# Five unread products around the first query products, an eight-fold Sinkhorn matrix, and a clearing that moves to a later round

## The chip, the cores and the metric

The kernel runs on one core of a Trainium2 chip. The metric is the device time of one execution in microseconds (us); the number given for a kernel is the median of its runs.

## The reference, cut to what matters

Four batches of eight heads, 768 positions, 64 values per head; `sort_net` holds one 8 by 8 matrix per batch and head.

```python
P = sort_net                                   # (4, 8, 8, 8)
for _ in range(5):
    P = exp(P - max(P, -1))
    P = P / (sum(P, -1) + 1e-9)
    P = P / (sum(P, -2) + 1e-9)
k_sorted = einsum('bhij,bhjcd->bhicd', P, k_blocks)     # 8 blocks of 96 positions
v_sorted = einsum('bhij,bhjcd->bhicd', P, v_blocks)
attn = softmax(q_blocks @ k_sorted.T / 8)               # 96 x 96 inside each block
x = (attn @ v_sorted)  ->  (3072, 512)
out = (silu(x @ w_gate) * (x @ w_val)) @ w_out          # 512 -> 1536 -> 512
```

## The kernel before, in words

The kernel has a short, latency-bound start and a long part in which TensorE (PE) works through the feed-forward blocks. Most of the order on PE, VectorE (DVE), ScalarE (ACT) and GpSimd (POOL) is the order in which the source issues the instructions: the start is under a manual schedule for these four, the rest under one for PE, POOL, ACT and SyncE.

**Sinkhorn** (L217 to L237). The 32 matrices lie on 32 partitions, `p_ps` is a tile in PSUM. A round is: the exponential on ACT (L219), then on DVE the row sum (L229), its reciprocal, the product (L231), the column sum (L232), its reciprocal, the product (L235). Each step needs the one before it, so DVE waits for ACT once in every round. Extra DVE and ACT work is put between the exponential and the row sum: the reduction to `mask` in the second round (L222), copies of V on ACT in the second to fourth (L223 to L227). In the last round the closing product writes `p_bf` (L236), a bf16 copy of the matrix, repeated four times along the free dimension. `vt_tile(pair)` (L192) allocates the tile for a pair of batches' mixed values and clears one column of it to 1.0 (L195); both tiles are made ahead of Sinkhorn.

**The mixing matrix** (L488 to L505). For each of the 8 output blocks, four products with a 32-column slice of `p_bf` as the stationary operand and the identity as the moving one write the transposed matrix to the four groups of 32 PSUM partitions of `w_ps` (L492). DVE multiplies it with `mask` into `rmix[0]` (L497) and copies the rest to `w_sb` (L502), from which POOL makes the other batches' `rmix`.

**Batch 0 on PE.** Ahead of `w_ps`, PE runs `wide_fill` (L481), fp32 products of zeros that nobody reads, with one tiny product between them that waits for a copy of V (L484), and then `q0_chunk(0, 0, 8)` (L274), the transposition of the first query pieces, which waits for their load. Behind `w_ps` come the other query pieces, the value products `v_chunk` (L300) and the key products `k0_chunk` (L284). Each of them fills one or two PSUM banks, which DVE or ACT then empties into SBUF (`drain`, L242 and L244). PSUM banks come from three rings: "gen" with three banks of 512 columns, "x" with one, and "a" and "b" with a pair each. Then follow scores (`qk`, L332) with the exponential on ACT (`e_all`, L345 and L343), `av` (L359) with its normalisation on DVE (L363, L365), the transposition of the result (L376), and the first gate and value products `early` (L557).

**The feed-forward blocks.** `ffn(n)` runs `gate` (L410), `value` (L428) and, for the block before, `outp` (L445); `merge` places the attention of later batches between them by fixed due times.

**Loads.** POOL issues them in program order: the first values, queries and keys, then its own copies of V into `vch` (L150), then the gate and value weights in pieces (`load_gv`, L136), then batch 1's keys, queries and values (L102) and the output weights (L514), then four more copies into `vch` for batch 1 (L150 again).

The fill that the start uses elsewhere, and that the change adds, is

```python
def fill(tile, n):
    for _ in range(n):
        nc.tensor.matmul(tile, lhsT=warm_sb[:, 0:128], rhs=warm_sb, start=True, stop=True)
```

where `warm_sb` is a 128 by 512 bf16 tile of zeros.

Of the kernel before, what the change touches and what calls it, by code (L numbers as in the profile page):

```python
# [10 lines left out]
BF16 = mybir.dt.bfloat16  # L11
AF = mybir.ActivationFunctionType
ALU = mybir.AluOpType
# [4 lines left out]
def kernel(  # L18
# [11 lines left out]
    nc = tc.nc  # L30

    B, H, S, D = q.shape
    NB = sort_net.shape[-1]
    C = S // NB
    BH = B * H
# [18 lines left out]
    const = ctx.enter_context(tc.tile_pool(name="const", bufs=1))  # L54
# [40 lines left out]
    def grouped(t):  # L95
        return t[:, :, 0:GC * D].rearrange("p s (c d) -> p s c d", d=D)

    def dense(t):
        return t.rearrange("p s n -> p (s n)")[:, 0:C * D].rearrange("p (c d) -> p c d", d=D)
# [42 lines left out]
    def copy_v(eng, pair, rows, s, n=4, d0=0, d1=D, cs=None):  # L142
        cs = cs or slice(s * (C // n), (s + 1) * (C // n))
        dst = vch3[rows, d0:d1, cs]
        src = (dense(v_tiles[0])[rows, cs, d0:d1] if rows == lowr else
               grouped(v_tiles[pair])[rows, s, :, d0:d1])
        if eng is nc.scalar:
            eng.copy(dst, src.transpose([0, 2, 1]))
        else:
            eng.tensor_copy(dst, src.transpose([0, 2, 1]))  # L150
# [41 lines left out]
    def vt_tile(pair):  # L192
        if pair not in vts:
            t = vtp.tile([C, 2, H * NB, D + 8], BF16, name=f"vt{pair}", tag="vt")
            nc.vector.memset(t[:, :, :, D:D + 1].rearrange("p u n e -> p (u n) e"), 1.0)  # L195
            vts[pair] = t
        return vts[pair]

    for pair in range(B // 2):
        vt_tile(pair)  # L200

    mask = const.tile([128, H], BF16)
    sel = const.tile([128, 2, H2, 16], BF16)
# [1 line left out]

    rowreds = [const.tile([BH, NB, 1], FP32, name=f"rowred{it}") for it in range(N_ITER)]
    colred = const.tile([BH, 1, NB], FP32)
    p_bf = const.tile([BH, NB, 4, NB], BF16)
    w_sb = const.tile([128, NB, B, H], BF16)
    pad = const.tile([1, 16], FP32)  # L210
    def pair_tile(name, tag):
# [2 lines left out]
    def bank_tile(name, tag="gen"):  # L214
        return psum.tile([128, 512], FP32, name=name, tag=tag, bufs=3 if tag == "gen" else 1)

    p_ps = bank_tile("p_ps")[0:BH, 0:NB * NB].rearrange("p (i j) -> p i j", j=NB)  # L217
    for it in range(N_ITER):
        nc.scalar.activation(p_ps, p_sb if it == 0 else p_ps, AF.Exp)  # L219
        if it == 1:  # L220
            with nc.allow_low_precision("0/1 mask"):
                nc.vector.tensor_reduce(mask, id4, axis=AX.XY, op=ALU.add)  # L222
            nc.scalar.copy(sel, ident.rearrange("p (r g two) -> p two g r", g=H2, two=2))  # L223
        if it == 2:
            copy_v(nc.scalar, 0, lowr, 0, cs=slice(24, 34))
        if it == 3:
            copy_v(nc.scalar, 0, lowr, 0, cs=slice(34, 46))  # L227
        rowred = rowreds[it]
        nc.vector.reduce_sum(rowred[:, :, 0], p_ps, axis=AX.X)  # L229
        nc.vector.reciprocal(rowred, rowred)  # L230
        nc.vector.tensor_mul(p_ps, p_ps, rowred.to_broadcast([BH, NB, NB]))  # L231
        nc.vector.reduce_sum(colred[:, 0, :], p_ps.transpose([0, 2, 1]), axis=AX.X)  # L232
        nc.vector.reciprocal(colred, colred)
        if it < N_ITER - 1:
            nc.vector.tensor_mul(p_ps, p_ps, colred.to_broadcast([BH, NB, NB]))  # L235
    nc.vector.tensor_tensor(p_bf, p_ps.unsqueeze(2).to_broadcast([BH, NB, 4, NB]),  # L236
                            colred.unsqueeze(1).to_broadcast([BH, NB, 4, NB]), op=ALU.mult)  # L237
    copy_v(nc.scalar, 0, lowr, 0, d1=40, cs=slice(46, 72))

    def drain(eng, dst, src):  # L240
        if eng == "v":
            nc.vector.tensor_copy(dst, src)  # L242
        else:
            nc.scalar.copy(dst, src)  # L244
# [3 lines left out]
    def kqt_tile(b):  # L248
        if b not in kqts:
            kqts[b] = kqp.tile([128, 2 * H2 * NB * C + 32], BF16, name=f"kqt{b}", tag="kqt")  # L250
        return kqts[b]
# [3 lines left out]
    def chunk_tile(name, n, tag):  # L255
        return pair_tile(name, tag) if n == 2 else bank_tile(name, tag)
# [12 lines left out]
    def q0_chunk(t, at, n, eng, tag):  # L269
        dst = kqt_tile(0)[:, GI * C:2 * GI * C].rearrange("p (g t r c) -> p t g r c", g=H2, t=2, c=QC)[:, t]  # L270
        tp = chunk_tile("tq0", n // 8, tag).rearrange("p (l g r) -> p l g r", l=n, g=H2)
        for lc in range(n):
            for two in range(2):
                nc.tensor.matmul(tp[two * D:(two + 1) * D, lc], lhsT=q0[t][:, at + lc, :],  # L274
                                 rhs=sel[:, two], start=True, stop=True)
        drain(eng, dst[:, :, :, at:at + n], tp.rearrange("p l g r -> p g r l"))
# [196 lines left out]
    idle_ps = bank_tile("idle_ps", "x")  # L473
# [5 lines that stand above are left out]
    def wide_fill(n):  # L479
        for _ in range(n):  # L480
            nc.tensor.matmul(idle_ps, lhsT=wide_sb[:, 0:128], rhs=wide_sb, start=True, stop=True)  # L481

    wide_fill(3)
    nc.tensor.matmul(idle_ps[0:8, 0:8], lhsT=vch[lowr, 24:32], rhs=vch[lowr, 24:32], start=True, stop=True)  # L484
    wide_fill(1)
    q0_chunk(0, 0, 8, "s", "x")

    w_ps = bank_tile("w_ps")[:, 0:NB * B * H].rearrange("p (i b h) -> p i b h", b=B, h=H)  # L488

    for i in range(NB):  # L490
        for g in range(4):
            nc.tensor.matmul(w_ps[32 * g:32 * g + 32, i].rearrange("p b h -> p (b h)"),  # L492
                             lhsT=p_bf[:, i].rearrange("p a b -> p (a b)"),
                             rhs=ident[0:BH, 0:BH], start=True, stop=True)

# [39 lines left out]
    idle_ps = bank_tile("idle_ps", "x")  # L535
# [159 lines left out]
```

## Time and profile before

| | |
|---|---|
| median of 3 runs | 245.98 us (245.24 to 246.05) |
| the profiled execution | 245.7 us, of which the span from first to last instruction is 243.9 us |
| PE busy | 235.5 us, 97% of the span |
| DVE, ACT, POOL busy | 155.6, 112.1, 54.6 us |
| mean granted clock of PE | 0.984 |

Times inside the profile count from the start of the span. "Idle before" is the time that an engine stood still ahead of an instruction, with what ended the wait. "PEclk" is the clock that PE was granted, as a share of the full one. A matmul's row includes the tail after its last column went in, so that two rows in sequence overlap a little; the spacing of a group is read from the chain of waits, which counts no time twice.

### The profile page before, as it was taken

To read this page: it belongs to the slowest core of one execution; us is meant where nothing else is said; L and a number is where in the kernel's file an instruction comes from. 1 tells how busy PE (TensorE), PEld (TensorE's weight loads), DVE (VectorE), ACT (ScalarE), POOL (GpSimd) and SP (SyncE) were. 2 spreads that over 40 slices of the span, in tenths; PEclk is the share of its full clock that TensorE was granted. 3 is DMA by queue.
4 is the path that set the end of the run, shared out by engine and by line. 5 is a ranking of instruction groups with operands and counts; after the bars stand their busy time and mean duration, and the time that the engine had idled before them with its cause. 6 is when DMAs were issued, how large, how long until landed. Compare 5 with 4: busy or idle time off the path is not lost.

```text
span 243.9 us, 5926 instructions
## 1 busy us (share of the span) xinstructions
PE 235.5 (97%) x2487; PEld 138.5 (57%) x2487; DVE 155.6 (64%) x327; ACT 112.1 (46%) x190; POOL 54.6 (22%) x66
## 2 busy tenths in 40 slices
PE   7598999999999999999999999999999999999994
PEld 3296666676555565555655555565556555555543
DVE  6668789876664585867755845574675576445700
ACT  3958654476635544455553452254325334332312
POOL 5997229970006089000000000000000000000000
PEclk9959999999999999999999999999999999999999
DMA  5989999999936998643121212012111211110122
GB/s 95 216 119 186 207 212 213 206 212 197 161 89 101 218 173 101 127 97 78 46 75 37 60 57 78 1 59 63 32 43 46 75 36 43 43 43 3 43 86 86
DMA packets 40698, 24.76 MB, mean 102 GB/s; under 512 B 29408, under 2 KB 35424, under 8 KB 40672
## 3 DMA queue, kind: packets, MB, share of 16 engines
q0 software_dynamic: 20688, 14.16, 39.9%
q1 hardware_dynamic: 19840, 10.17, 16.0%
q8 instruction: 19, 0.31, 0.5%
q10 hardware_dynamic: 144, 0.07, 0.1%
q14 instruction: 7, 0.06, 0.1%
HBM read 28.32 MB, written 7.86 MB: 148 GB/s over the span
## 4 chain that ended last, share of the span: by engine, by line
PE 92%; DVE 4%; ACT 1%; DMA 1%; issue 1%
PE v_ps L428 25%; PE g_ps L410 25%; PE o_ps L445 25%; PE av_ps L359 3%; PE tkq L264 3%; PE qk L332 3%; PE tv L300 2%; PE tk L284 1%; PE tv L310 1%; PE o_ps L461 1%; PE tq L274 1%; DMA p_sb<-in_sort_net_dram 1%; PE g_ps L557 1%; DVE st L365 1%; PE x_ps L376 1%
## 5 line engine op out<-in xcount | busy, mean ns | idle before, releaser
L420 DVE SCALAR_TENSOR_TENSOR gs_sb<-th_sb,g_ps 128x384 bf16<-128x384 bf16 x96 | 52.9, 551 | 50.0 <-ACT th_sb L418 46.9
L410 PE MATMUL g_ps<-xt,wg_sb 128*128 128x384 bf16 x376 | 76.6, 326 | 0.1
L428 PE MATMUL v_ps<-xt,wv_sb 128*128 128x384 bf16 x376 | 76.5, 326 | 0.0
L418 ACT ACTIVATE th_sb<-g_ps 128x384 bf16<-128x384 f32 x96 | 47.1, 491 | 56.8 <-PE g_ps L410 54.1
L445 PE MATMUL o_ps<-wo,h 128*128 128x512 bf16 x276 | 64.4, 379 | 0.0
L433 DVE SCALAR_TENSOR_TENSOR h<-v_ps,gs_sb 128x384 bf16<-128x384 f32 x96 | 53.4, 556 | 7.7 <-DVE gs_sb L420 0.5
L410 PEld LDWEIGHTS <-wg_sb 128*128 128x128 bf16 x376 | 34.8, 97 | 23.4
L428 PEld LDWEIGHTS <-wv_sb 128*128 128x128 bf16 x376 | 35.0, 97 | 23.1 <-issue 0.2
L445 PEld LDWEIGHTS <-h 128*128 128x128 bf16 x276 | 26.0, 98 | 28.5
L450 ACT COPY o_sb<-o_ps 128x512 f32<-128x512 f32 x23 | 13.5, 586 | 49.3 <-PE o_ps L445 46.3
L150 POOL COPY vch<-v 64x1536 bf16<-64x1536 bf16 (+2 forms) x11 | 29.1, 2688 | 9.9 <-DMA v<-in_v_dram 9.9
L345 ACT ACTIVATE e_all<-qk 96x768 bf16<-96x768 f32 x30 | 23.2, 801 | 3.8 <-PE qk L332 3.7
L365 DVE TENSOR_TENSOR st<-av_ps,r_sb 96x512 bf16<-96x512 f32 x32 | 21.7, 680 | 0.3
L359 PEld LDWEIGHTS <-e_all 96*128 96x128 bf16 x256 | 11.9, 97 | 4.6 <-ACT e_all L345 0.3
L359 PE MATMUL av_ps<-vt,e_all 96*128 96x65 bf16 x256 | 13.0, 193 | 0.2 <-ACT e_all L345 0.2
L244 ACT CAST vt<-tv 96x1024 bf16<-96x1024 f32 (+1 forms) x10 | 9.7, 965 | 5.9 <-PE tv L310 3.5
L363 DVE RECIPROCAL r_sb<-av_ps 96x8 f32<-96x8 f32 x32 | 6.3, 198 | 7.8 <-PE av_ps L359 7.8
L242 DVE CAST vt<-tv 96x1024 bf16<-96x1024 f32 (+1 forms) x8 | 8.1, 1017 | 3.1 <-PE tv L310 1.8
L481 PE MATMUL idle_ps<-wide_sb 128*128 128x512 f32 x8 | 6.6, 977 | 1.5 <-DVE wide_sb L70 1.5
L242 DVE COPY oq_v<-o_ps 128x128 f32<-128x128 f32 x1 | 0.3, 291 | 9.3 <-PE o_ps L461 9.3
L300 PE MATMUL tv<-rmix,vch 64*128 64x64 bf16 (+1 forms) x128 | 5.8, 208 | 0.0
L300 PEld LDWEIGHTS <-vch 64*128 64x128 bf16 (+1 forms) x128 | 5.4, 107 | 0.6
(87 smaller groups left out, 132.9 us busy)
## 6 DMA issues: line engine op xcount, KB each, us to landing
out_dram<-o_sb SPq DMA_DIRECT2D x23, 256.0 KB, 2.0
v<-in_v_dram POOLq DMA_DIRECT2D x4, 384.0 KB, 11.8
wo<-in_moe_w_out_dram POOLq DMA_DIRECT2D x3, 512.0 KB, 17.3
kqp<-in_k_dram POOLq DMA_DIRECT2D x2, 768.0 KB, 10.7
q_scr<-in_q_dram POOLq DMA_DIRECT2D x2, 768.0 KB, 18.1
v<-in_v_dram POOLq DMA_DIRECT2D x2, 768.0 KB, 9.8
wg_sb<-in_moe_w_gate_dram POOLq DMA_DIRECT2D x2, 512.0 KB, 12.0
wv_sb<-in_moe_w_val_dram POOLq DMA_DIRECT2D x2, 512.0 KB, 14.2
```

The costliest lines, as they stand in the source:

```text
L150: eng.tensor_copy(dst, src.transpose([0, 2, 1]))
L300: nc.tensor.matmul(tp[:, ld, :], lhsT=vch[rows, col:col + 128], rhs=mix, start=True, stop=True)
L345: nc.scalar.activation(e_all[:, n:n + 2, 0:4 * C], wide[0:C, :, 0:4 * C], AF.Exp, scale=scale)
L359: nc.tensor.matmul(o[:, two, i4, 0:D + 1], lhsT=e[:, i4 * C:i4 * C + 128], rhs=vt[:, 2 * g + two, half * 4 + i4, 0:D + 1], start=True, sto ...
L365: nc.vector.tensor_tensor(st.rearrange("p i two d -> p two i d"), o[0:C, :, :, 0:D], r_sb.to_broadcast([C, 2, 4, D]), op=ALU.mult)
L410: nc.tensor.matmul(g_ps, lhsT=wg_sb[:, kc, ts(m, 128)], rhs=xt[:, kc, :], start=(kc == 0), stop=(kc == NKC - 1))
L418: nc.scalar.activation(th_sb, g_ps, AF.Tanh, scale=0.5)
L420: nc.vector.scalar_tensor_tensor(gs_sb, th_sb, 1.0, g_ps, op0=ALU.add, op1=ALU.mult)
L428: nc.tensor.matmul(v_ps, lhsT=wv_sb[:, kc, ts(m, 128)], rhs=xt[:, kc, :], start=(kc == 0), stop=(kc == NKC - 1))
L433: nc.vector.scalar_tensor_tensor(h_tiles[n][:, m, :], v_ps, 0.5, gs_tiles.pop(m), op0=ALU.mult, op1=ALU.mult)
L445: nc.tensor.matmul(o_ps, lhsT=h_w[:, m, ts(t3, 128)], rhs=wo_sb[part][:, m % 4, :], start=(m == 0), stop=(m == NFC - 1))
L450: nc.scalar.copy(o_sb, o_ps)
```

## The change

Three edits, all in the start. Three products of 512 columns are issued on PE ahead of the first query products and two behind them, the latter into a bank of the "gen" ring; nobody reads what they write. `p_bf` holds the matrix eight times instead of four, so a stationary operand has 64 columns, and each output block takes two products that write 64 partitions each instead of four that write 32. The tile for the second pair of batches is made, and its column cleared, in Sinkhorn's third round and no longer ahead of the first.

```diff
-    for pair in range(B // 2):
-        vt_tile(pair)
+    vt_tile(0)
...
-    p_bf = const.tile([BH, NB, 4, NB], BF16)
+    p_bf = const.tile([BH, NB, 8, NB], BF16)
...
         if it == 2:
             copy_v(nc.scalar, 0, lowr, 0, cs=slice(24, 34))
+            vt_tile(1)
...
-    nc.vector.tensor_tensor(p_bf, p_ps.unsqueeze(2).to_broadcast([BH, NB, 4, NB]),
-                            colred.unsqueeze(1).to_broadcast([BH, NB, 4, NB]), op=ALU.mult)
+    nc.vector.tensor_tensor(p_bf, p_ps.unsqueeze(2).to_broadcast([BH, NB, 8, NB]),
+                            colred.unsqueeze(1).to_broadcast([BH, NB, 8, NB]), op=ALU.mult)
...
     wide_fill(1)
+    fill(idle_ps, 3)
     q0_chunk(0, 0, 8, "s", "x")
+    fill(bank_tile("idle_ps"), 2)
...
     for i in range(NB):
-        for g in range(4):
-            nc.tensor.matmul(w_ps[32 * g:32 * g + 32, i].rearrange("p b h -> p (b h)"),
+        for g in range(2):
+            nc.tensor.matmul(w_ps[64 * g:64 * g + 64, i].rearrange("p b h -> p (b h)"),
                              lhsT=p_bf[:, i].rearrange("p a b -> p (a b)"),
                              rhs=ident[0:BH, 0:BH], start=True, stop=True)
```

## The prediction

> **What bounds the kernel now.** I read the page first, then the granted clock by stretches, then the chain that ended last, then the timelines of DVE, PE and POOL in the first 50 us. The page:
>
> ```profile
> span 243.9 us, 5926 instructions
> ...
> PE 235.5 (97%) x2487; PEld 138.5 (57%) x2487; DVE 155.6 (64%) x327; ACT 112.1 (46%) x190; POOL 54.6 (22%) x66
> ...
> PEclk9959999999999999999999999999999999999999
> ```
>
> TensorE (PE) is busy nearly throughout, so time that is taken out of the start reaches the end unless a later load stops it. The one odd digit is the 5 in the third slice of the clock. The windows view, cut at the clock's own steps, shows it (columns: stretch, its length, then busy time and count of PE, PEld, DVE, ACT, POOL, then granted clock, DMA share, GB/s):
>
> ```profile
> 7.54:10.95 3.41, 1.66 (x19) 0.71 (x19) 2.56 (x13) 3.23 (x5) 3.41 (x2) 1.00 1.10 222
> 10.95:14.36 3.41, 3.03 (x96) 2.93 (x97) 2.18 (x6) 2.07 (x3) 3.41 (x4) 0.51 0.52 106
> 14.36:17.78 3.42, 3.42 (x112) 3.27 (x110) 2.36 (x5) 2.54 (x4) 3.42 (x6) 0.50 1.16 151
> 17.78:21.19 3.41, 2.80 (x64) 2.07 (x63) 2.76 (x6) 2.37 (x4) 3.21 (x7) 0.99 1.17 183
> ```
>
> PE ran at half clock for 6.83 us, from 10.95 to 17.78. The stretch that went before had PE busy for 1.66 of 3.41 us (49%); a stretch with 2.80 of 3.41 us (82%) kept the full clock. So I read a grid of 3.41 us, a drop after a stretch that is too idle, and a hold limit somewhere between 49% and 82%. Where PE idled in the bad stretch stands in its timeline:
>
> ```profile
> 7.80 1.12 PE L481 MATMUL idle_ps<-wide_sb 128*128 128x512 f32 x2
> 10.01 0.44 PE L274 MATMUL tq<-sel,qk 128*64 128x64 bf16 x16 [1.08 <-DMA qk<-in_q_dram]
> 11.33 0.40 PE L492 MATMUL w_ps<-ident,p_bf 32*32 32x32 bf16 x32 [0.88 <-DVE p_bf L236]
> ...
> 19.63 0.35 PE L332 MATMUL qk<-kqt 64*128 64x96 bf16 x8 [0.35 <-DVE vt L242]
> ```
>
> Two gaps, 1.08 us until the query load lands and 0.88 us until Sinkhorn's last product: the five new products are put in these two. What the half clock costs stands in the chain of waits (start, length, work):
>
> ```profile
> 11.73 1.00 PE tq L274 x31
> 12.73 2.24 PE tv L300 x40
> 14.97 2.70 PE tk L284 x96
> 17.68 0.88 PE tv L300 x24
> 19.32 0.82 ACT e_all L345
> ...
> 26.34 0.88 PE tq L274 x48
> ...
> 44.13 1.13 PE tkq L264 x64
> ...
> 130.01 2.59 PE o_ps L445 x12
> ```
>
> From 11.73 to 18.56 the path is PE alone, at half clock. The same L274 products take 32 ns each at half clock (1.00 over 31) and 18 ns at full (0.88 over 48); L284 takes 28 ns, and its twin L264 at full clock 18 ns.
>
> **The change, part by part.**
>
> *Five fills.* A warm product of 512 columns takes 0.216 us (L445, 2.59 over 12). Three after 8.92 (the end of the row at 7.80) end by 9.57, before the query data at 10.01: hidden by that load. If the clock were already low they would take twice that, 1.3 us, and hold L274 up by 0.2 us. Two after 10.45 end at 10.88, hidden by the wait for p_bf; cold, they would end some 0.1 us behind it. In the stretch 7.54 to 10.95 PE is then busy for 1.66 + 5 x 0.216 = 2.74 us, 80%, next to the 82% that held. So I take it that the clock is not lowered at 10.95. The second fill takes one more turn of the three-bank "gen" ring, but what it wrote nobody reads, so it delays no one.
>
> *Sinkhorn.* From the DVE timeline and the chain:
>
> ```profile
> 2.83 0.36 DVE rowred L229
> ...
> 4.67 0.22 DVE rowred L229
> ```
>
> ```profile
> 3.02 0.17 DVE L195 MEMSET vt<- 96x128 bf16 x1
> ...
> 4.34 0.26 DVE L222 TENSOR_REDUCE mask<-ident 128x8 bf16<-128x128 bf16 x1
> ...
> 9.20 0.22 DVE L235 TENSOR_TENSOR p_ps<-p_ps,colred 32x64 f32<-32x64 f32 x1
> ...
> 10.87 0.41 DVE L236 TENSOR_TENSOR p_bf<-p_ps,colred 32x256 bf16<-32x256 f32 x1
> ...
> 12.31 0.36 DVE L502 CAST w_sb<-w_ps 128x192 bf16<-128x192 f32 x1
> ...
> 18.36 1.22 DVE L242 CAST vt<-tv 96x1024 bf16<-96x1024 f32 x1 [0.22 <-PE tv L300]
> ```
>
> The clearing at 3.02 lies inside round one's row sum, which takes 0.36 us there and 0.22 in round two; with it gone, 0.0 to 0.2 us is gained, and I take 0.15. In round three it goes into the gap in which DVE waits for the exponential. In round two the longer mask reduction (0.26 us) sits in that gap and the row sum starts right behind the exponential, so it costs nothing; were the gap not there, 0.17 us. The last product grows from 256 to 512 columns: from 0.22 at 64 and 0.41 at 256, 1.0 ns a column, so +0.26, and p_bf is ready at 11.29 - 0.15 + 0.26 = 11.40. The mixing products fall from 32 to 16, each twice as wide: at full clock between half of their 0.40 us and 16 x 18 = 0.29 us; I take 0.3, the row of the nearer shape. They end at 11.7, as before. Without the clock these edits together are worth -0.2 to +0.3 us.
>
> *What the full clock brings.* PE's 0.6 times shorter work isn't all gain, since DVE and ACT empty each bank. The groups between 11.3 and 20.3 us (busy time, mean ns, then idle time before them):
>
> ```profile
> L242 DVE CAST vt<-tv 96x512 bf16<-96x512 f32 (+1 forms) x4 | 3.2, 816 | 1.3 <-PE tv L300 1.3
> ...
> L242 DVE CAST kqt<-tk 128x256 bf16<-128x256 f32 (+1 forms) x5 | 2.5, 526 | 0.6 <-PE tk L284 0.6
> ```
>
> DVE idles 1.3 + 0.6 = 1.9 us in them for PE. It ends the cast at 19.58 (18.36 + 1.22), on which the second score product waited (0.35 us). With PE quick, DVE waits 0.1 us for the first products and then runs on: 1.8 us earlier, 17.8. The first scores need neither that cast nor its bank: PE's work from 11.7 on is 32 + 96 products at 18 ns and 64 at about 29 ns (from the row at 51.03 below: 0.63 us, less 0.16 for the tail of its last product, over 16), 4.2 us; with waits of 0.7 us for banks PE comes to them at 16.6 and the first e_all starts at about 17.1 instead of 19.32, 2.2 us earlier. The second exponential follows the first on ACT in both kernels, so I take 2.1 us (1.8 to 2.3) at the attention's start. What could be late on the way is block 0's key load: its second half is issued some 0.5 us behind 3.50 and takes at most 9.7 us to land, about 13.7, while PE would be ready for it at 13.4; DVE still has the value casts to do until 14.6, so that 0.3 us is covered.
>
> ```profile
> 3.50 1.09 POOL L175 DMA_DIRECT2D qk<-in_k_dram  x2
> ```
>
> ```profile
> DMA to landing us min/median/max: 7.0/7.7/9.7
> ```
>
> *What is late next.* POOL's loads don't move with PE: they are queued behind its own copies. So PE runs towards them:
>
> ```profile
> 18.78 0.81 POOL L136 DMA_DIRECT2D wv_sb<-in_moe_w_val_dram  x1
> ...
> 29.60 0.59 POOL L102 DMA_DIRECT2D kq<-in_q_dram  x1 [1.95 <-DMA wv_sb<-in_moe_w_val_dram]
> ```
>
> ```profile
> 37.91 11.21 POOL L150 COPY vch<-v 64x1536 bf16<-64x1536 bf16 x4
> ```
>
> ```profile
> 31.21 0.82 PE L428 MATMUL v_ps<-xt,wv_sb 128*128 128x384 bf16 x4
> ...
> 51.03 0.63 PE L300 MATMUL tv<-rmix,vch 128*128 128x64 bf16 x16
> ```
>
> The third value-weight load (columns 512 to 1023, first used by the L428 group at 31.21) let POOL go on at 29.60, so it had landed by then: slack 1.6 us, some 0.2 more because POOL starts a little behind a landing. The copies of block 1's values end at 49.12 and are first read at 51.03: slack 1.9. So of the 2.1 us about 1.8 goes through (1.6 to 1.9), and the rest is spent waiting for value weights at about 29.3. Behind that PE is packed and everything moves up.
>
> **Sum.** The profiled execution took 245.7 us, 1.8 over its span of 243.9; less 1.8 it is 243.9. It lies 0.28 below the median of the runs shown, 245.98; for the median I give 245.98 - 1.8 = 244.2.
>
> **The rivals.** About 0.3%, 0.74 us, is what a measurement can tell from no change: faster is under 245.24, slower over 246.72.
>
> *A: the clock holds to the end*, as above: 243.7 to 244.7. For it: 80% beside a held 82%. Chance 0.60.
>
> *B: only part of it is there to win.* The steps at 7.54, 10.95, 14.36 and 17.78 are a grid; should it lie elsewhere in other executions, the half clock of before would end earlier in them and less is gained: the runs reach from 245.24 to 246.05. Or a load is later than I read it. A gain of 0.5 to 1.3, 245.0. Chance 0.13. The Trainium skill, "TensorE: Matmul & The Clock Gate", section on the clock gate, says that this window is free-running and that the cold stretch varies from run to run; one trace can't show that.
>
> *C: the fills don't hold the clock*, the limit being above 80%, or another measure than busy time (the fills multiply zeros). Then the Sinkhorn edits alone count, -0.2 to +0.3: 246.0. Chance 0.14. The same page, in its table of goals, asks only that no idle gap exceed about 3 us; by that rule the 1.08 and 0.88 us gaps would have cost no clock and the fills would be needless, 246.0. The trace disagrees: the clock fell at 10.95 with no gap over 1.08 us.
>
> *D: the drop moves into the attention.* With PE quick, it waits for banks between 14.36 and 17.78: of 3.42 us it would idle about 0.17 + 0.35 for banks and some more for casts, 78 to 85% busy. If the limit lies there, the clock falls at 17.78 for two stretches, as it did before, and they hold the scores and then the packed early gate products: about 1.2 us in the first (0 to 1.7) and 1.7 in the second, 2.9 against the 2.1 won: 246.8 (245.6 to 247.3). It decides once that stretch falls under the hold limit. Against it: 17.78:21.19, with 82%, held. Chance 0.13.
>
> **Numbers.** The range takes A, B and the lower half of C: 243.5 to 246.0; alone, A is 243.7 to 244.7. Faster: A and nearly all of B, 0.70; same: C and the rest, 0.17; slower: D, 0.13.
>
> **What would show it.** Right: one granted clock of 1.00 from 7.54 to the end; p_bf with 0.67 us; the first e_all near 17.1; DVE's idle time before its casts almost gone; a PE wait for wv_sb of some 0.3 us near 29.3. Wrong: a 0.5 at 10.95 (C) or at 17.78 (D); an e_all before 17.5 with the same end (loads hold back more than I read).

## The result and the profile after

The changed kernel takes 244.68 us in the median of 22 runs (243.93 to 246.19), the kernel before 245.86 over as many (245.19 to 248.47); the ratio is 0.9951, with a 95% interval of 0.9929 to 0.9974. The profiled execution took 243.93 us with a span of 242.2, where before it was 245.7 and 243.9.

The page of the profile after, its span and its clock row:

```profile
span 242.2 us, 5881 instructions
...
PEclk9999999999999999999999999999999999999999
```

The 5 in the third slice is gone. The windows of the changed kernel, cut at its own clock steps (which lie 1.1 us earlier than in the profile before), with PE's busy time as the second number and the granted clock third from the end:

```profile
6.46:9.87 3.41, 2.18 (x7) 0.67 (x6) 2.56 (x13) 3.33 (x5) 3.41 (x2) 1.00 1.07 214
9.87:13.28 3.41, 2.88 (x98) 2.28 (x99) 2.59 (x9) 2.73 (x3) 3.41 (x3) 1.00 0.84 172
13.28:16.70 3.42, 3.15 (x135) 2.93 (x131) 3.28 (x7) 2.64 (x6) 3.42 (x6) 1.00 0.81 102
16.70:20.11 3.41, 2.60 (x61) 2.10 (x61) 2.95 (x7) 3.18 (x6) 3.41 (x5) 1.00 1.15 173
```

The full clock stays. PE's timeline shows the fills in the two gaps and the products behind them at the full clock: 96 key products in 1.93 us, where they took 2.77.

```profile
8.62 0.81 PE L477 MATMUL idle_ps<-warm_sb 128*128 128x512 bf16 x3
9.89 0.44 PE L274 MATMUL tq<-sel,qk 128*64 128x64 bf16 x16 [0.46 <-DMA qk<-in_q_dram]
10.26 0.60 PE L477 MATMUL idle_ps<-warm_sb 128*128 128x512 bf16 x2
11.37 0.42 PE L494 MATMUL w_ps<-ident,p_bf 32*64 32x32 bf16 x16 [0.51 <-DVE p_bf L236]
...
13.84 1.93 PE L284 MATMUL tk<-rmix,qk 128*64 128x64 bf16 x96
```

DVE now runs through its casts with hardly a gap, and ACT's first exponential of the attention starts 2.0 us earlier, at 17.34 (DVE's and ACT's timelines):

```profile
12.80 1.88 DVE L242 CAST vt<-tv 96x512 bf16<-96x512 f32 x3
14.60 1.64 DVE L242 CAST kqt<-tk 128x512 bf16<-128x512 f32 x3
16.38 1.22 DVE L242 CAST vt<-tv 96x1024 bf16<-96x1024 f32 x1
```

```profile
17.34 1.51 ACT L345 ACTIVATE e_all<-qk 96x768 bf16<-96x768 f32 x2
```

The chain that ended last no longer follows Sinkhorn. It begins with V's load, goes through POOL's copies and queue and reaches PE through a weight load (start, length, work):

```profile
6.26 6.81 POOL vch L150 x3
...
17.27 12.12 DMA wv_sb<-in_moe_w_val_dram
29.39 0.04 issue
29.44 0.82 PE v_ps L428 x4
```

A simple sum holds from here on. From the start of the first e_all to the end of the span it is 243.9 - 19.32 = 224.6 us before, and 242.0 - 17.42 = 224.6 in a profile of the changed kernel in which no load was waited for (`after_copy`, below). What is over 224.6 in another profile is a wait behind that point: in the one above 242.16 - 17.34 = 224.8 (the span unrounded), so 0.2 us.

### The profile page after: what moved, and what is told of

Same layout as the page of the kernel before. It is cut to its first block, busy times and chain, and to the rows that moved or that the text cites. A ratio compares the mean times of both kernels' runs of the same rounds, so it can differ in the third digit from the quotient of the medians.

```text
span 242.2 us, 5881 instructions
## 1 busy us (share of the span) xinstructions
PE 232.7 (96%) x2453; PEld 136.8 (56%) x2476; DVE 155.6 (64%) x327; ACT 112.0 (46%) x190; POOL 54.9 (23%) x66
## 4 chain that ended last, share of the span: by engine, by line
PE 85%; DMA 7%; POOL 5%; issue 1%; DVE 1%; ACT 0%; POOLq 0%
PE v_ps L428 25%; PE g_ps L410 25%; PE o_ps L445 24%; DMA wv_sb<-in_moe_w_val_dram 5%; POOL vch L150 3%; PE tkq L264 3%; PE av_ps L359 3%; PE qk L332 2%; DMA v<-in_v_dram 2%; PE tv L310 1%; PE o_ps L461 1%; POOL wg_sb L136 1%; PE tv L300 1%; POOL wv_sb L136 1%; PE x_ps L376 0%
## 5 line engine op out<-in xcount | busy, mean ns | idle before, releaser
L445 PE MATMUL o_ps<-wo,h 128*128 128x512 bf16 x254 | 61.4, 379 | 1.5 <-issue 0.5
L395 POOL DMA_DIRECT2D q_scr<-in_q_dram x2 | 5.6, 2813 | 0.3 <-issue 0.3
L332 PE MATMUL qk<-kqt 64*128 64x96 bf16 x128 | 4.5, 204 | 0.7 <-PE tv L300 0.4
```

Source lines behind the costliest of these rows:

```text
L445: nc.tensor.matmul(o_ps, lhsT=h_w[:, m, ts(t3, 128)], rhs=wo_sb[part][:, m % 4, :], start=(m == 0), stop=(m == NFC - 1))
```

## The experiments

Theory: the five fills keep the clock up, that alone carries the gain, and a load then holds back part of it. Rivals: the Sinkhorn edits carry it; TensorE alone sets the end; fewer fills would do.

### The fills alone, and all but the fills

```diff
 # fills_only: the kernel before, and
+    fill(idle_ps, 3)
     q0_chunk(0, 0, 8, "s", "x")
+    fill(bank_tile("idle_ps"), 2)
 # no_fills: the changed kernel without these two lines
```

> The kernel before with the five fills alone (four-fold Sinkhorn matrix, both clearings ahead of round one). Clock theory: the fills carry the whole gain; granted clock 1.00 over 10.95 to 17.78, first e_all at 17.0 to 17.4 (19.32 before, 17.34 in the changed kernel), time 1.2 to 1.9 us under the kernel before. Rival (the wider Sinkhorn products or the moved clearing carry it): first e_all after 18.5, time within 0.7 us of the kernel before.

> The changed kernel without its five fills, so the eight-fold matrix and the moved clearing alone. Clock theory: the clock falls to 0.5 near 11 us as in the kernel before and stays there for about 6.8 us; first e_all 19.0 to 19.6; time within -0.2 to +0.3 us of the kernel before. Rival: a gain of over 0.7 us with the clock down.

`fills_only`: 244.77 us, median of 12 (ratio 0.9976, 0.9950 to 1.0002: its own interval just reaches 1; its median lies 1.1 us under the 245.90 of the kernel before). The profile is plain: full clock throughout, first e_all at the same 17.34. Behind it PE waited 0.36 us for the value weights. The group starts 0.77 us behind the one ahead of it (28.98), where `after_copy` has 0.25, and that is the 0.5 in the span of 242.5 = 17.34 + 224.6 + 0.5:

```profile
29.75 0.82 PE v_ps L428 x4
```

```profile
PE v_ps L428 <- DMA wv_sb<-in_moe_w_val_dram: 0.4, 1, 0.4
```

`no_fills`: 246.48 us (1.0038, 1.0005 to 1.0070), 0.6 us over the median of the kernel before. The clock fell, and the first e_all came at 19.84 (the page, then the chain of waits):

```profile
PEclk9959999999999999999999999999999999999999
```

```profile
17.46 1.39 PE tv L300 x24
19.84 0.81 ACT e_all L345
```

So the fills carry the whole gain; the kernel with the Sinkhorn edits and without them loses. That loss was outside what I had expected (-0.2 to +0.3), and so was the first e_all (19.0 to 19.6). How much of it is the edits' own is not shown: the mixing rows on DVE started at 11.94, 0.1 us later than before (11.83). In this profile the half clock began at 12.5 us and not at 11.0, and so lasted into the last value products (24 in 1.39 us): the place of the clock's steps differs from one execution to the next, and with it the time. Another 0.6 us of the span, 245.07 - 19.84 - 224.6, is waiting behind the attention's start, most of it for a transposing transfer of the attention's result, which no edit of the change touches:

```profile
76.07 0.32 PE L410 MATMUL g_ps<-xt,wg_sb 128*128 128x384 bf16 x1 [0.47 <-DMA xt<-st]
```

### Three fills, or two

```diff
 # fills_3_0: the changed kernel without "fill(bank_tile("idle_ps"), 2)"
 # fills_0_2: the changed kernel without "fill(idle_ps, 3)"
```

> The changed kernel with the three early fills alone, none behind the first query products. Worked out from the stretches of 3.41 us: the idlest one has TensorE busy for about 1.66 + 3 x 0.216 = 2.3 us, 68%. If the hold limit is under 65% (the idlest stretch that held in the changed kernel, 2.22 of 3.41 us), the clock stays up: first e_all 17.3 to 17.6, time within 0.4 us of the changed kernel. If all five are needed: a 0.5 in the granted clock, first e_all after 18.5, time within 0.7 us of the kernel before.

> The changed kernel with the two late fills alone. The idlest stretch has 1.66 + 2 x 0.216 = 2.1 us, 61%, or less, since the gap of 1.08 us ahead of the query load stays open. Limit between 49% and 61%: the clock holds, first e_all 17.3 to 17.6. Limit at 61% or more: a 0.5 between 10 and 19 us, first e_all after 18.5, time 0.7 us or more over the changed kernel.

`fills_3_0`: 245.94 us (0.9987, 0.9966 to 1.0009). `fills_0_2`: 246.48 (1.0025, 0.9999 to 1.0052). Single runs tell more than the medians, since each comes with its mean granted clock. With three fills, the two runs at a clock of 1.0 took 244.35 and 244.40 us, and the four at 0.985 or 0.986 took 246.06 to 246.51; of the other four, three at 0.990 to 0.993 took 244.21 to 245.81 and one at 0.972 took 248.33. With two fills, one run of seven kept the clock (244.48); the others, five at 0.985 or 0.986 and one at 0.979, took 246.16 to 247.09. With all five, 41 of 46 runs have 0.997 or more. In both profiles the clock fell, and the first e_all came at 19.70 and 19.77. So each group of fills is wanted, and what they change is how many executions keep the clock; that the place of the steps decides for the rest is the reading that fits, and wasn't tested.

The stretches of 3.41 us ahead of the drops, `fills_3_0` first, then `fills_0_2`; of each kernel the first stretch kept the clock and the second lost it:

```profile
4.98:8.40 3.42, 1.91 (x6) 0.66 (x5) 2.58 (x13) 2.31 (x4) 2.15 (x1) 1.00 1.00 199
8.40:11.81 3.41, 1.90 (x41) 0.94 (x40) 2.39 (x10) 3.33 (x4) 3.41 (x3) 1.00 1.07 218
```

```profile
5.39:8.80 3.41, 1.88 (x5) 0.38 (x3) 2.47 (x13) 2.55 (x4) 2.34 (x1) 1.00 1.00 200
8.80:12.22 3.42, 1.94 (x61) 1.19 (x62) 2.39 (x10) 3.08 (x4) 3.42 (x3) 1.00 1.08 221
```

1.91 and 1.88 us of busy time kept it, 1.90 and 1.94 lost it. There is no one limit in PE's busy time: the first stretches hold almost only wide products of 512 columns on the whole array, the second ones two or three of these and then products of 64 and 32 columns on a half or an eighth of it. That such products count for less is the reading that fits; it wasn't measured by itself. The kept traces support it without settling it. Take all stretches at the full clock in the first 27 us of the fourteen profiles, and weigh each product's time by the share of the 128 by 128 array that it uses (fills whose record is missing are counted in): the seven stretches ahead of a drop hold 0.6 to 1.65 us, those that kept the clock 1.45 and more. In plain busy time the two kinds overlap from 1.88 to 2.7 us.

### The loads that are late next

```diff
 # loads_first: the changed kernel, and in POOL's order
-    copy_v(nc.gpsimd, 0, lowr, 0, d0=40, cs=slice(46, 72))
     load_gv(0, 256)
+    copy_v(nc.gpsimd, 0, lowr, 0, d0=40, cs=slice(46, 72))
 # before_loads: the same edit on the kernel before
 # after_copy, after_copy2: the changed kernel; loads_first2: loads_first again
```

> The changed kernel once more, as the partner of the next one on the same chip. Load theory: its runs spread over 1 to 2 us at a full clock, and its fifth value group (line 428, near 29 us) starts on the landing of wv_sb; 1.0 to 1.8 us under the kernel before. Rival (the spread is the clock's): the slower runs have a mean granted clock under 0.995.

> The changed kernel, with the first two weight loads of POOL issued ahead of its third copy of V instead of behind it. Load theory: the loads behind them land about 1.2 us earlier, the wait for wv_sb near 29.4 is gone, the end is 0.2 to 0.6 us earlier than in the changed kernel, and the spread of its runs shrinks to that of the kernel before (0.9 us or less). Rival (TensorE alone sets the end): within 0.2 us of the changed kernel, the same spread. If the late copy holds the value products (line 300, from column 40 of D), the first e_all comes later than 17.34.

> The changed kernel again, as the partner of the three below. Load theory: at a full clock its runs reach from about 243.9 to over 245.5, as in the 32 such runs so far; two of 34 so far showed a mean clock under 0.995.

> The changed kernel with the first two weight loads ahead of POOL's third copy, once more. Load theory: all runs with a mean clock of 0.997 or more lie between 243.9 and 244.8, none above. If that was chance, a third or more of them lie above 244.8. On the clock: its four drops in 12 runs were chance if at most one run of this set has a clock under 0.995, the edit's own doing if three or more have.

> The kernel before with only the two weight loads moved ahead of the third copy. Loads have 1.6 us of slack there, so: no change, first e_all 19.3 to 19.9, within 0.4 us of the kernel before. If the loads bound that kernel too, 0.7 us or more faster.

The medians don't move: 244.44 and 244.61 us for the changed kernel (0.9946, 0.9921 to 0.9971; 0.9948, 0.9920 to 0.9975), 244.50 and 244.43 for `loads_first` (0.9946, 0.9911 to 0.9981; 0.9928, 0.9890 to 0.9967). What was expected of the median, 0.2 to 0.6 us, is not there. The first e_all of the two `loads_first` profiles came at 17.59 and 17.76, later than 17.34. That was to be the sign of a copy that holds the value products, but the copy had ended by 14.66 and 14.53, over 1 us before those products began (15.79 and 15.86); what delayed them stays open. `before_loads` is at 245.86 (0.9974, 0.9929 to 1.0018), with the first e_all at 19.39, so the loads did not bind before, as I had read.

The single runs say where it went. At a clock of 0.997 or more, the changed kernel's runs reach from 243.81 to 246.19 us, 15 of 41 above 244.8. With the loads moved they reach from 243.71 to 244.82, one of 16 above 244.8; the two kernels further below that also have them moved, `best4` and `best5`, add none of 16. So the spread at a full clock is not the clock's. In a profile the wait is gone, since POOL goes on behind the third value-weight load at 28.65, and at 29.68 in the changed kernel (POOL's timelines, `loads_first`, then the changed kernel):

```profile
28.65 0.59 POOL L102 DMA_DIRECT2D kq<-in_q_dram  x1 [1.96 <-DMA wv_sb<-in_moe_w_val_dram]
```

```profile
29.68 0.59 POOL L102 DMA_DIRECT2D kq<-in_q_dram  x1 [2.44 <-DMA wv_sb<-in_moe_w_val_dram]
```

So the order of the loads is behind the long runs at a full clock: the edit that lets them land earlier removes those. That this very load is the late one in each of the long runs stays open: none of the profiles taken is of such a run. Another candidate is the transposing transfer seen in `no_fills`: in the profile of `clear_pool` (below), at the full clock, PE waits 0.22 us for it.

But eight of the 24 runs with the moved loads have a clock below 0.995, where five of 46 have it without. Four of them are in the second set of twelve; three or more there were to mean that the edit itself does it. The profile of `loads_first2` is one of them, and in it the clock fell for one stretch of the attention:

```profile
15.88:19.29 3.41, 2.37 (x60) 1.94 (x58) 2.60 (x6) 2.25 (x4) 3.41 (x5) 1.00 1.18 188
19.29:22.71 3.42, 3.42 (x45) 2.65 (x44) 2.59 (x7) 2.54 (x6) 3.16 (x23) 0.50 1.34 187
```

The stretch ahead of the drop shows 2.37 us of work, where the changed kernel shows 2.60. Neither number is complete: the trace has the weight load of the fill ahead of the first scores, at 16.92 here, but not its product. With some 0.3 us for that it is 2.7 us, and the changed kernel's stretch, into which its fill reaches for 0.2 us, comes to 2.8. The first e_all was at 17.76 and the span 243.3 us, so the stretch at half clock cost 243.3 - 17.76 - 224.6 = 0.9 us. What the moved loads win in the long runs they lose by this; how the moved loads make the clock fall more often is not settled.

### The clearing out of Sinkhorn

```diff
 # clear_pool: the changed kernel, and
-            vt_tile(1)                       # in round three, VectorE
+    vt_tile(1, nc.gpsimd)                    # behind the mixing rows, GpSimd
```

> The changed kernel with the second clearing on GpSimd, behind Sinkhorn, and none in round three. If the clearing costs round three 0.18 us (reciprocal 0.64 us behind the exponential's start there, 0.46 in the other rounds), the mixing rows on VectorE start 0.18 us earlier, about 11.7, the first e_all about 17.2, and the end moves up by 0.1 to 0.2 us unless a load waits. If the clearing is hidden in the gap: no change, 11.84 to 11.94 and 17.4.

The median is 244.44 us (0.9950, 0.9933 to 0.9967), that of the changed kernel. The 0.18 us of round three is real. In the changed kernel DVE's row sum takes 0.36 us there and the reciprocal comes at 6.36, 0.64 behind the exponential's start at 5.72; without the clearing it comes at 6.29, 0.47 behind the start at 5.82:

```profile
5.95 0.36 DVE L229 TENSOR_REDUCE rowred<-p_ps 32x8 f32<-32x64 f32 x1 [0.26 <-ACT p_ps L218]
6.13 0.17 DVE L195 MEMSET vt<- 96x128 bf16 x1
6.36 0.19 DVE L230 RECIPROCAL rowred<-rowred 32x8 f32<-32x8 f32 x1
```

```profile
6.04 0.21 DVE L228 TENSOR_REDUCE rowred<-p_ps 32x8 f32<-32x64 f32 x1 [0.25 <-ACT p_ps L218]
6.29 0.19 DVE L229 RECIPROCAL rowred<-rowred 32x8 f32<-32x8 f32 x1
```

Yet p_bf's product began at 10.58 and in the changed kernel at 10.64; the mixing rows started at 11.78 and the first e_all at 17.28, 0.06 us earlier each, and not 0.18. Round four's exponential stands behind ACT's first copy of V, and that copy waits for V's load. `clear_pool`, ACT's timeline: the copy ends at 7.47 and the exponential follows at 7.49.

```profile
6.20 1.27 ACT L148 COPY vch<-v 64x640 bf16<-64x640 bf16 x1 [0.19 <-DMA v<-in_v_dram]
7.49 0.19 ACT L218 ACTIVATE p_ps<-p_ps 32x64 f32<-32x64 f32 x1
```

So up to round three Sinkhorn has little left to win: V's landing and a copy of 1.3 us set round four.

### All that looked good, together

```diff
 # best4: the kernel before, with the five fills, the second clearing on GpSimd,
 # the two weight loads ahead of the third copy, and without
-    fill(pair_tile("idle_ps", "a")[:, 0:512], 1)
     qk(0, 0, "a")
 # best5: best4 with that line put back
```

> The kernel before with the five fills and a four-fold matrix, the second clearing on GpSimd, the first two weight loads ahead of POOL's third copy of V, and without the fill ahead of the first scores. If e_all's start sets the end (span = start of the first e_all + 224.6 us, which fits the kernel before and the three undisturbed profiles of the changed one), the mixing rows start at about 11.4, the first e_all at 16.7 to 17.0 and the span is 241.3 to 241.7, the time 0.4 to 0.8 us under the changed kernel's own profile. If the third copy holds the value products: first e_all at 17.3 or later and no gain. If the clock falls for want of the removed fill: 0.5 near 17 to 20 us and a time of 245 or more.

> The last version with the fill ahead of the first scores put back: five fills, four-fold matrix, second clearing on GpSimd, two weight loads ahead of the third copy. Runs at a full clock 243.7 to 244.4 as without that fill; if the missing fill was why five of 12 runs lost the clock, now at most two of 12 do, and the median falls to about 244.0, 0.4 under the changed kernel's. If the fill has nothing to do with it: again a third or more under 0.995.

`best4`: 244.14 us (0.9950, 0.9919 to 0.9982); `best5`: 244.38 (0.9924, 0.9891 to 0.9957). Neither is told apart from the changed kernel, whose own interval is 0.9929 to 0.9974. At a clock of 0.997 or more both are quick and even: 243.60 to 244.21 us (7 of 12) and 243.60 to 244.62 (9 of 12). The rest lost the clock and took 245.43 to 249.03 us in `best4`; in `best5` 246.36, 249.68 and, in one run at a mean clock of 0.657, 344.5. Whether the fill put back helps isn't shown: 3 of 12 are below 0.995 beside 5 of 12, between the two outcomes that I had set apart. The first e_all of `best4` was at 17.46, and not near 16.9, for two reasons. V landed late in that execution, DVE waited in round four, and the mixing rows started at 11.74 and not at 11.4:

```profile
7.93 0.21 DVE L228 TENSOR_REDUCE rowred<-p_ps 32x8 f32<-32x64 f32 x1 [0.62 <-ACT p_ps L218]
```

Then PE stood still for block 0's keys, and its last value products, and with them ACT's last cast ahead of the first e_all, came behind these (PE's timeline):

```profile
14.05 2.09 PE L283 MATMUL tk<-rmix,qk 128*64 128x64 bf16 x96 [0.35 <-DMA qk<-in_k_dram]
```

The third copy, the reason that I had named for an e_all at 17.3 or later, had ended at 14.97, before the products that need it (16.07). In `best5` PE waits 0.30 us for the same keys. So the key load, which the prediction had found covered by DVE's casts, is the next wait once Sinkhorn gets shorter.

The profile of `best5` is of a run in which the clock fell in the attention for two stretches. Rival D of the prediction is here to be seen:

```profile
15.43:18.84 3.41, 2.23 (x61) 1.86 (x57) 2.61 (x5) 2.04 (x4) 3.41 (x6) 1.00 1.21 197
18.84:22.25 3.41, 3.41 (x53) 2.75 (x51) 2.33 (x6) 2.61 (x7) 3.15 (x18) 0.50 1.33 171
22.25:25.67 3.42, 3.42 (x20) 1.89 (x18) 1.50 (x4) 0.69 (x2) 2.01 (x10) 0.50 1.24 205
```

The record of the fill ahead of the first scores is missing here too; with it the stretch ahead of the drop has some 2.5 us of work. The span is 244.56 with the first e_all at 17.63, so the two stretches cost 2.3 us.

## Why the prediction was right, point by point

**The clock.** Right, and the whole gain: with the fills alone the first e_all is at 17.34 as in the full change, without them at 19.84. In the stretch that I had looked at, 7.54 to 10.95, PE was busy for 2.85 us, where I had worked out 2.74. But the grid lay elsewhere, and the idlest stretch on it had 2.18 us. And the limit in busy time "between 49% and 82%" on which I leaned doesn't exist as such: 1.88 us (55%) was kept, 1.94 lost, and in `loads_first2` 2.37 lost (69%, and nearly 80% with the fill whose record is missing). The outcome was right; the comparison of 80% with 82% was no ground for it, so that part was luck. Nor can it be read from busy time why five fills hold in 41 of 46 runs and three in 2 of 10.

**The attention's start.** 2.0 us earlier (17.34 for 19.32), where I took 2.1 with 17.1. PE came to the scores at 16.95 and not at 16.6. The work that I had summed up was done by about 16.6; what I had left out is the fill ahead of the scores. In `after_copy`, where its record is kept, it begins at 16.59 and the scores follow at 17.04:

```profile
16.59 0.39 PE L477 MATMUL idle_ps<-warm_sb 128*128 128x512 bf16 x1
17.04 0.35 PE L332 MATMUL qk<-kqt 64*128 64x96 bf16 x8
```

**The next wait.** Right in place and nearly in size for the profiled run: the value weights at 29.44 (I gave 29.3), about 0.2 us of waiting where I had 0.3, and 1.8 us through to the end, as forecast. Two errors of 0.1 us cancel in that: the attention came 2.0 us earlier and not 2.1. The row that I showed for the load, at 18.78, is the fourth value-weight load; the third is issued at 17.32, as the row 17.27 of the chain after shows for the changed kernel. The sum went by POOL's start at 29.60, so nothing in it hung on that row. It is a wait in some executions only: in `after_copy` PE was at that point at 29.31 and did not wait.

**The median.** I took the profile's 1.8 us off the median of before and got 244.2; measured are 244.68, a gain of 1.2, inside the range but at the edge of what rival A alone allowed (243.7 to 244.7). The step that was too simple is this one. The changed kernel's profiled run is its shortest, and 11 of its 22 runs lie within 0.6 us of it; the 11 others take 0.9 to 2.3 us more, two of them at a clock of 0.991 and 0.992, nine at the full clock. I had put "a load is later than I read it" into rival B, at 245.0 and a chance of 0.13. By the runs with the moved loads, which lack these nine's like, it seems to hold for some two fifths of the runs: with the slack of 1.6 to 1.8 us used up, a late load reaches the end, and it did not before.

**Sinkhorn's edits.** "As before" for the mixing rows was right (11.84 beside 11.82 in `fills_only`), by three errors that nearly cancel. The clearing costs 0.18 us in round three, where I gave it nothing, on the evidence of the mask reduction, which does hide there. And it gave more in round one than the 0.15 I took: in `fills_only` the reciprocal comes at 3.24 although the exponential began at 2.38; in the changed kernel at 2.84 with a start at 2.35, 0.40 earlier. p_bf's product takes 0.68 us, as worked out, and p_bf is ready at 11.32 (I gave 11.40). The 16 wider products take 0.42 us by their row and not 0.3, so they do not pay it back: DVE waits 0.52 us for them, and 0.54 for the 32 narrow ones at the full clock in `fills_only`.

**Rivals.** C (nothing but the edits) is refuted by `fills_only`. D did not happen in the profiles of the changed kernel, but its mechanism exists: two variants show it, at 0.9 us for one stretch and 2.3 for two, where I had 1.2 and 2.9. It may be behind the few runs of the changed kernel with a clock near 0.992; no profile of one was had.

## What to carry to other kernels

Idle gaps of a microsecond ahead of dense work cost TensorE half its clock for the 7 us behind them here, and in the attention of two variants a stretch of small products whose gaps were all under 0.4 us was followed by 3.4 and 6.8 us of half clock too. Unread products in gaps that end with a load or another engine cost nothing here and held it in most executions; judge them over many runs by the mean clock of each, since whether a gap matters depends on where the clock's grid falls. When a stage gets shorter, list the loads that do not move with it and their slack: once it is used up, their scatter becomes the kernel's.

## What the runs showed of the hardware

The grid of 3.41 us lies differently from execution to execution: the first steps are at 6.46 and 6.37 us in two profiles of the changed kernel and at 7.58 in that of the kernel before (where the prediction's cuts are 0.04 us early). A stretch at half clock takes 0.5 x 3.41 of some 244 us, 0.007, off the mean clock, and the mean clocks of single runs cluster accordingly. The kernel before has runs near 0.993 (one stretch, 244.59 to 244.65 us), near 0.985 (two, most of them 245.3 to 246.1), near 0.978 (three, 245.7 to 246.1) and, fewer, at 0.972 and 0.965 (247.8 to 248.5). The profiles agree: one stretch at 0.993 in `loads_first2`, two at 0.984 in the kernel before.

The clearing of one column of a tile (96 partitions by 128 strided elements) takes 0.17 us on VectorE, but it starts 0.4 us behind the end of its predecessor, with nothing in the profile that holds it: ahead of round one (2.07 to 2.47) and in round three (5.69 to 6.13). A mask reduction of 0.26 us in the same kind of gap starts at once and is hidden; the clearing is not. Why the clearing starts late was not looked into.
